# First batch of an attention + two-layer kernel written as one list of steps, with other load layouts, other PSUM places and regrouped norms for batches 1 and 2

## The chip, the cores and the metric

The kernel runs on one core of a Trainium2 chip. The metric is the device time of one execution in microseconds (us). Engines are named as in the profile: PE (TensorE), PEld (its weight loads), DVE (VectorE), ACT (ScalarE), POOL (GpSimd) and SP (SyncE, which here only issues DMAs). An engine takes its instructions strictly in the order in which the program lists them for that engine, and the kernel fixes that order by hand.

## What is computed

Eight batches of attention with 12 heads, 448 positions and head width 64, with q and k normalised by their root mean square, and after it two dense layers with a GELU between them:

```python
q_n, k_n = rmsnorm(q, g_q), rmsnorm(k, g_k)
attn = softmax(scale * q_n @ k_n.transpose(0, 1, 3, 2))
x = (attn @ v).transpose(0, 2, 1, 3).reshape(8 * 448, 768)
out = gelu_tanh(x @ w_in) @ w_out          # 768 -> 2048 -> 768
```

Inputs and outputs are float32 in HBM; the matmuls run in bf16.

## The kernel before, in words

**Tiling.** A batch's 12 heads are 6 pairs, and the pairs are 3 chunks of 4 heads (`c` = 0, 1, 2). Per chunk the kernel loads q and k (`load_q` L106, `load_k` L122, on SP's queue), squares them (`square` L164), sums the squares per row (`total` L192, DVE), takes the inverse root as exp(-0.5 ln) on ACT (`rsqrt` L195), multiplies (`normed` L209, on DVE or POOL) and transposes. A transpose is either four plus three or four TensorE transposes per pair (`trans` L221) whose results DVE copies out of PSUM, with k multiplied by the gains, or two DMA transposes per chunk (`dma_trans` L248) with a DVE multiply behind them (`gain` L260).

Keys are cut into 128-row tiles: three per head, and the last 64 keys of a head share a tile with another head's. So a pair has 3 score tiles, and each chunk one tile "r" more: 7 per chunk, 21 per batch. `scores` (L265) does two matmuls (four for "r") into a PSUM place of two banks, and one exp on ACT. There are three such places, which the first layer also uses. `pair_products` (L306) multiplies the exps by ones (what = 0, the softmax sums) and by v (what = 1); both write the single PSUM bank `o`. `pair_recips` (L326) turns the sums into reciprocals with two DVE transposes and a reciprocal, `pair_x` (L335) multiplies. For batches from 1 on, DVE first adds the exps of a pair (`key_sum` L291), so that the sums need 2 matmuls; for batch 0 they need 8.

The first layer (`mm1` L349) makes 16 blocks of 128 features in 6 steps each, two blocks to a PSUM place, with one GELU on ACT per place (L368). The second layer (`mm2` L376) runs in steps, 16 per output half tile; `attention` (L451) interleaves them as fills between the score tiles of the next batch, in 7 groups of three score tiles. After batch 0 there are 96 such steps, after later batches 112 on average.

**Order of the work.** `first_attention` (L514) runs batch 0's 21 score tiles with lists of side work per tile (L661 to L681). Its sums and products share the bank `o`, so that pair after pair goes sums, reciprocals, products, multiply. The transposes use the bank `mm`. Then come `first_blocks` (L496) and the rest of the first layer of batch 0; between them `between0` (L701) finishes batch 1's sums of squares, takes the inverse roots of the whole of batch 1 and loads the GELU table. Lines L713 to L720 norm batch 1 on DVE and transpose chunk 0 and chunk 2 on TensorE (`trans(1, 0)`, `trans(1, 1)`, `trans(1, 4)`, `trans(1, 5)`) and chunk 1 by DMA (`transposed(1, 1)`). In `attention(1)` POOL squares batch 2's chunks 1 and 2 and DVE sums those of all three (L721 to L727). The loop from L709 does the same for later batches, with POOL norming (`normed_all`) and DMA transposes for all chunks.

POOL's queue also issues the casting loads: v (`load_v` L139, six DMAs a batch), w_in in two parts (L609) and w_out in two halves (L615). SP's queue issues the q and k loads, the DMA transposes and the stores.

Of the kernel before, what the change touches and what calls it, by code (L numbers as in the profile page):

```python
# [16 lines left out]
def kernel(  # L17
# [34 lines left out]
    rawqk = ctx.enter_context(tc.tile_pool(name="rawqk", bufs=4))  # L52
    stp = ctx.enter_context(tc.tile_pool(name="stp", bufs=2))
    smp = ctx.enter_context(tc.tile_pool(name="smp", bufs=4))
    nrmp = ctx.enter_context(tc.tile_pool(name="nrmp", bufs=3))
# [6 lines left out]
    ps_s = ctx.enter_context(tc.tile_pool(name="ps_s", bufs=3, space=bass.MemoryType.PSUM))  # L62
    ps_o = ctx.enter_context(tc.tile_pool(name="ps_o", bufs=1, space=bass.MemoryType.PSUM))
    ps_m = ctx.enter_context(tc.tile_pool(name="ps_m", bufs=1, space=bass.MemoryType.PSUM))

# [21 lines left out]

    vb = [wts.tile([128, NCH, 2, NS, D], BF16, name=f"vb{i}") for i in range(2)]
    vr = [wts.tile([128, 2, NCH, 2, D], BF16, name=f"vr{i}") for i in range(2)]
# [27 lines left out]
    def halves(j):  # L117

        own, other = slice(64 * j, 64 * j + 64), slice(64 - 64 * j, 128 - 64 * j)
        return ((own, slice(0, 256), 4, 3 * j), (other, slice(256, S), 3, 4 * j))  # L120

    def load_k(b, c):  # L122
        t = rawqk.tile([128, 2, NS, D], F32, tag="rawk", name="rawk")
        raws["k", b, c] = t

        def go(j):
            h = head(c, j)
            for p, s, n, at in halves(j):
                nc.sync.dma_start(  # L129
                    t[p, :, at:at + n],  # L130
                    k[b, h:h + 2, s].rearrange("a (p t) d -> p a t d", t=n),
                )
        return [lambda j=j: go(j) for j in range(2)]

    def loads(b, c):
        for go in load_q(b, c) + load_k(b, c):
            go()

    def load_v(b, j, cs=slice(0, NCH)):  # L139
        src = v[b, HP * j + 2 * cs.start:HP * j + 2 * cs.stop]  # L140
        dst, rem = vb[b % 2], vr[b % 2]
        for p, s, n, at in halves(j):
            nc.gpsimd.dma_start(
                dst[p, cs, :, at:at + n].rearrange("p c a t d -> p (c a) (t d)"),
                src[:, s].rearrange("h (p t) d -> p h (t d)", t=n),
            )
        p, s, n, at = halves(j)[0]
        nc.gpsimd.dma_start(
            rem[p, j, cs].rearrange("p c a d -> p (c a) d"),
            src[:, s].rearrange("h (p t) d -> p h t d", t=n)[:, :, 3 - 3 * j],  # L150
        )
# [12 lines left out]
    def square(b, c, n, eng, part=None):  # L164
        if (n, b, c) not in sqs:
            sqs[n, b, c] = sq_tile(n, stp.tile([128, CH * NQ * D], F32, tag="sq", name="sq"))
# [54 lines left out]
    def trans(b, hp):  # L221

        c, j = hp // 2, hp % 2
        if hp == 0:
            qT[b] = qkp.tile([128, HP, S], BF16, tag="qT", name="qT")
        tp = ps_m.tile([128, 2, 512], BF16, tag="mm", name="tp")
        for t in range(NQ):
            nc.tensor.transpose(
                tp[:, 0, t * P:(t + 1) * P],
                nrms["q", b, c][:, j, t].rearrange("p a d -> p (a d)"), ident[:P, :P],  # L230
            )
        s = slots(j)
        n = s.stop - s.start
        for i in range(n):
            nc.tensor.transpose(
                tp[:, 1, i * 128:(i + 1) * 128],
                nrms["k", b, c][:, s.start + i].rearrange("p a d -> p (a d)"), ident,
            )
        if b == 0 and hp == 0:
            nc.scalar.copy(qT[b][:, hp], tp[:, 0, :S])  # L240
        else:
            nc.vector.tensor_copy(qT[b][:, hp], tp[:, 0, :S])
# [565 lines left out]
```

## Time and profile before

| what | us |
|---|---|
| three runs: median (lowest, highest) | 435.16 (433.12, 435.74) |
| the profiled execution | 437.02 |
| its span, first to last instruction | 434.9 |
| PE busy, share of the span | 414.1 (95%) |
| ACT, DVE, POOL busy | 286.1, 265.4, 160.6 |
| first score tile of batch 0 on PE | 9.10 |
| first matmul of the first layer, batch 0 | 39.55 |
| first score tile of batch 1 | 66.76 |
| start of the first layer of batch 1 | 101.24 |
| the same for batches 2 and 3 | 149.58, 197.92 |

The last five rows are read in the timeline of PE. They cut the run into stages: start, batch 0's attention, batch 0's first layer, batch 1's attention with batch 0's second layer inside, and then one period per batch. A period is 48.34 us long. A busy PE says little by itself, since fillers on zeros count as busy and a matmul at half the clock counts twice as long; the granted clock stands beside it.

### The profile page before, as it was taken

The page shows a single profiled execution, that of the slowest core. Times are in us where ns is not written, and L with a number is a line of the kernel's source. Part 1 is how long each engine was busy: PE and PEld are TensorE (multiplying, and loading weights), DVE is VectorE, ACT ScalarE, POOL GpSimd, SP SyncE. Part 2 cuts the span into 40 slices and gives each one's busy share as a digit, 9 for nine tenths or more (in the row PEclk, how much of TensorE's full clock was granted, in tenths as well). Part 3 has the DMA queues.
Part 4 walks back from the last instruction along what each step waited for, and adds up shares of the span by engine and source line. Part 5 has one row for each costly group of instructions (what it writes and reads, how often), then busy time and mean ns, then how long its engine had stood idle before and what let it go on. Part 6 is the DMA issues. An engine that isn't in the chain of part 4 may idle for free.

```text
span 434.9 us, 9265 instructions
## 1 busy us (share of the span) xinstructions
PE 414.1 (95%) x3776; PEld 236.4 (54%) x3776; DVE 265.4 (61%) x441; ACT 286.1 (66%) x382; POOL 160.6 (37%) x181
## 2 busy tenths in 40 slices
PE   8778798899999999999999999999999999999996
PEld 3234454456555565556465655556565655556563
DVE  5577846798667844787267845877377821784010
ACT  5676538366787758767786859777786648674400
POOL 4979223254660094205560194206560280000000
PEclk9899999699999999999999999999999999999999
DMA  7999999665895158913994168914991162120022
GB/s 177 217 228 233 231 179 230 124 110 95 206 194 107 38 128 170 217 51 73 208 186 102 38 150 160 217 43 78 220 142 39 38 110 56 36 69 7 2 72 72
DMA packets 90505, 54.92 MB, mean 126 GB/s; under 512 B 51808, under 2 KB 85472, under 8 KB 90464
## 3 DMA queue, kind: packets, MB, share of 16 engines
q1 hardware_dynamic: 65248, 41.67, 42.9%
q0 software_dynamic: 24896, 12.59, 21.9%
q8 instruction: 29, 0.48, 0.4%
q10 hardware_dynamic: 320, 0.10, 0.1%
q14 instruction: 12, 0.10, 0.1%
HBM read 47.19 MB, written 11.01 MB: 134 GB/s over the span
## 4 chain that ended last, share of the span: by engine, by line
PE 79%; DMA 13%; DVE 5%; SPq 2%; issue 1%; ACT 0%; DVEq 0%
PE o L386 32%; PE hh L362 26%; PE o L321 10%; PE sc L285 6%; DMA rawk<-in_k_dram 6%; DMA rawq<-in_q_dram 4%; PE h L362 3%; DMA kT<-nrmk 3%; PE sc L275 1%; SPq L129 1%; DVE ss L193 1%; DVE es L301 1%; DVE es L299 1%; SPq L110 1%; DVE nrmq L216 0%
## 5 line engine op out<-in xcount | busy, mean ns | idle before, releaser
L386 PE MATMUL o<-wout,g 128*64 128x384 bf16 (+1 forms) x1664 | 159.7, 329 | 0.0
L289 ACT ACTIVATE ex<-sc,shift 128x896 bf16<-128x896 f32 x144 | 136.6, 1013 | 8.5 <-PE sc L285 8.4
L362 PE MATMUL hh<-xT,win 128*64 128x448 bf16 (+1 forms) x960 | 135.3, 355 | 2.7 <-ACT g L368 2.6
L386 PEld LDWEIGHTS <-g 128*64 128x64 bf16 (+1 forms) x1664 | 99.4, 110 | 50.6 <-issue 4.6
L362 PEld LDWEIGHTS <-win 128*64 128x64 bf16 (+1 forms) x1098 | 88.1, 106 | 61.5 <-issue 8.2
L368 ACT ACTIVATE g<-hh 128x896 bf16<-128x896 f32 x56 | 49.6, 917 | 55.0 <-PE hh L362 55.0
L193 DVE TENSOR_REDUCE ss<-sq 112x16 f32<-112x1024 f32 (+4 forms) x44 | 46.8, 1077 | 39.9 <-ACT sq L176 32.7
L408 ACT COPY osb<-o 128x384 f32<-128x384 f32 x51 | 24.7, 485 | 59.5 <-PE o L386 59.5
L331 DVE STREAM_TRANSPOSE st<-o 128x448 f32<-128x448 f32 x48 | 31.2, 649 | 29.4 <-PE o L321 29.3
L654 POOL COPY mark<-es 1x1 bf16<-1x1 bf16 x6 | 1.1, 178 | 127.0 <-DVE es L301 127.0
L216 POOL TENSOR_TENSOR nrmq<-rawq,rinv 112x512 bf16<-112x512 f32 x40 | 41.7, 1060 | 3.1 <-ACT rinv L202 3.1
L285 PE MATMUL sc<-qT,kT 64*128 64x448 bf16 x288 | 38.6, 355 | 1.4 <-DVE kT L243 0.9
L321 PE MATMUL o<-ex,vb 128*64 128x448 bf16 x288 | 36.9, 363 | 1.0 <-DVE st L331 0.8
L301 DVE TENSOR_TENSOR es<-ex 128x896 bf16<-128x896 bf16 x42 | 27.7, 659 | 15.4 <-ACT ex L289 15.2
L216 POOL TENSOR_TENSOR nrmk<-rawk,rinv 128x384 bf16<-128x384 f32 (+1 forms) x40 | 36.8, 936 | 0.0
L338 DVE TENSOR_TENSOR xT<-o,rb 128x448 bf16<-128x448 f32 x48 | 29.6, 617 | 4.4 <-PE o L321 3.5
L178 POOL TENSOR_TENSOR sq<-rawq 112x1024 f32<-112x1024 f32 x9 | 17.4, 1929 | 39.9 <-DMA rawq<-in_q_dram 25.8
L333 DVE STREAM_TRANSPOSE rb<-rc 128x448 f32<-128x448 f32 x48 | 31.0, 645 | 1.6
L299 DVE TENSOR_TENSOR es<-es,exr 64x896 bf16<-64x896 bf16 x42 | 27.4, 653 | 3.0 <-ACT exr L289 1.6
L301 DVE TENSOR_TENSOR es<-es,ex 128x896 bf16<-128x896 bf16 x42 | 27.1, 645 | 2.4 <-ACT ex L289 0.3
L261 DVE TENSOR_SCALAR kT<-kT,gcol 128x896 bf16<-128x896 bf16 x19 | 15.4, 813 | 21.4 <-DMA kT<-nrmk 21.4
L289 ACT ACTIVATE exr<-sc,shift 128x896 bf16<-128x896 f32 x24 | 24.5, 1021 | 0.2 <-PE sc L275 0.2
(71 smaller groups left out, 318.4 us busy)
## 6 DMA issues: line engine op xcount, KB each, us to landing
rawq<-in_q_dram SPq DMA_DIRECT2D x48, 224.0 KB, 4.2
rawk<-in_k_dram SPq DMA_DIRECT2D x48, 128.0 KB, 4.5
rawk<-in_k_dram SPq DMA_DIRECT2D x48, 96.0 KB, 4.4
vb<-in_v_dram POOLq DMA_DIRECT2D x16, 192.0 KB, 6.0
win<-in_moe_w_in_dram POOLq DMA_DIRECT2D x2, 1536.0 KB, 16.9
wout<-in_moe_w_out_dram POOLq DMA_DIRECT2D x2, 1536.0 KB, 21.8
out_dram<-osb SPq DMA_DIRECT2D x7, 336.0 KB, 3.9
vb<-in_v_dram POOLq DMA_DIRECT2D x16, 144.0 KB, 6.7
```

Of the source, the lines that this page charges most:

```text
L193: nc.vector.reduce_sum(stat(ssq[b % 3], b, c, n, j), view(n, sqs[n, b, c], j), axis=AX.X)
L216: eng.tensor_mul(dst.rearrange("p t a d -> p a t d"), view(n, raws[n, b, c], j), r.to_broadcast(list(r.shape) + [D]),)
L285: nc.tensor.matmul(sc[:, a, :S], kT[r, c, 4 * j + t], qT[b][r, hp], start=True, stop=True,)
L289: nc.scalar.activation(dst, sc[:, :, :S], AF.Exp, scale=scale, bias=shift)
L299: nc.vector.tensor_add(es[p], es[p], exrs[b, hp // 2][p])
L301: nc.vector.tensor_add(es, ex[:, 0] if t == 1 else es, ex[:, t])
L321: nc.tensor.matmul(o[a * D:(a + 1) * D], w(a), e[:, a], start=(i == 0), stop=(i + 1 == len(steps)),)
L331: nc.vector.transpose(st.rearrange("p a b -> p (a b)"), oas[0])
L333: nc.vector.transpose(oas["rb"], rc.to_broadcast([128, S // 32, 32]))
L362: nc.tensor.matmul(h[i * m:(i + 1) * m, j, :S], win[:, c // 2 + NCH * (c % 2), f * 128 + i * m:f * 128 + (i + 1) * m], xT[b][:, c], start= ...
L368: nc.scalar.activation(g[:, fs[0]:fs[0] + len(fs), (b % 2) * S:(b % 2 + 1) * S], h[:, :, :S], AF.Gelu_apprx_tanh)
L386: nc.tensor.matmul(o[j * m:(j + 1) * m, :HD], g[:, f, i * 128 + j * m:i * 128 + (j + 1) * m], wout[:, f, half * HD:(half + 1) * HD], start ...
```

## The change

In batch 0 and up to the end of its first layer, the code that ordered the work (`first_attention`, its side lists, `between0`, the batch-0 lists L713 to L720) is replaced by one string of steps, `FRONT`, which a function `front` walks through. A step names its work and, after a colon, its engine (A, D, P for ACT, DVE, POOL). `s3` is the matmuls of score tile 3, `e3` its exp, `sq`/`sk` squares, `tq`/`tk` row sums, `rs` inverse roots, `nq`/`nk` norms, `tpq`/`tpk` transposes, `cq`/`ck` their copies out of PSUM, `su`, `st`, `rc`, `rb`, `xp`, `xt` a pair's sums, the three parts of the reciprocals, the products and the multiply, `ma`/`mc`/`md` parts of the first layer, `g` a GELU, `v`, `w`, `o`, `L` loads, and capitals the same for batch 1. `z` is filler matmuls.

- **PSUM.** Batch 0 has two score places instead of three; the other two banks take its q and k transposes (`tpq`, `tpk`). At step `U` these two banks become the third score place. Its products go to the bank `mm` and its sums to the bank `o`.
- **Loads.** k comes as 384 rows on 128 partitions (pieces of 768 bytes) and the last 64 rows on 64 partitions (pieces of 256 bytes); before it was 256 rows on 64 partitions (1024 bytes) and 192 on the other 64 (768 bytes). q is loaded as before. v takes three DMAs a batch instead of six. In POOL's queue v and both parts of w_in stand directly behind two small operations of the start. w_out comes in four parts.
- **Batch 1.** Inverse roots for chunks 0 and 1 are taken inside batch 0's first layer, between two more table loads; chunk 0 is transposed into the banks `o` and `mm`, chunk 1 into two score places (`TP2`, `TP3`) at the end of the first layer. Chunk 2's inverse roots come after it, its norms on DVE behind the first three score tiles of `attention(1)`, and its transposes by DMA, with `gain(1, 2)` at the end of group 3.
- **Batch 2.** Its squares, sums, inverse roots and norms move: chunk 0 squared by ACT in groups 5 and 6 of `attention(1)`, chunks 1 and 2 in batch 1's first layer, with two table loads and the inverse roots there; all norms on DVE. Batch 3's squares of chunks 1 and 2 go to ACT in `attention(2)`.
- **Pools.** Squares have four buffers of their own, norms two instead of three, the reciprocal's first transpose one instead of two.

```diff
-    nrmp = ctx.enter_context(tc.tile_pool(name="nrmp", bufs=3))
+    nrmp = ctx.enter_context(tc.tile_pool(name="nrmp", bufs=2))
-    ps_s = ctx.enter_context(tc.tile_pool(name="ps_s", bufs=3, space=bass.MemoryType.PSUM))
+    ps_s = ctx.enter_context(tc.tile_pool(name="ps_s", bufs=2, space=bass.MemoryType.PSUM))
+    ps_t = tc.tile_pool(name="ps_t", bufs=1, space=bass.MemoryType.PSUM)
+    turn = [ps_t.__enter__()]
...
+        def main(j):
+            h = head(c, j)
+            nc.sync.dma_start(
+                t[:, :, 4 * j:4 * j + NK],
+                k[b, h:h + 2, :SM].rearrange("a (p t) d -> p a t d", t=NK),
+            )
+        def last(j):
+            h = head(c, j)
+            nc.sync.dma_start(t[own(j), :, NK], k[b, h:h + 2, SM:].rearrange("a p d -> p a d"))
...
+    def third():
+        ps_t.__exit__(None, None, None)
+        pool = ctx.enter_context(tc.tile_pool(name="ps_u", bufs=1, space=bass.MemoryType.PSUM))
+        turn.extend([pool, ps_s, ps_s])
...
+        elif name == "TP":
+            tp = place("tp").rearrange("p a s -> p (a s)").bitcast(BF16)
+            tps["Q", i], tps["K", i] = (
+                trans(1, i, n, tp[:, 1024 * a:1024 * (a + 1)]) for a, n in enumerate("qk"))
...
+    FRONT = """
+        sq0:A tq0 sk0:A tk0 sq1:P gcol rs0 shift nq0:P tq1 sk1:A tk1 tpq0 sq2:A v0 nk0:D rs1 cq0:D
+        tpk0 tq2 sk2:A z3 v1 ck0:A tk2 v2 s0 nk1:D rs2 s1 w0 nq1:D e0 tpk1 sk3:D w1 tpq1 e1 s2 tk3
+        z5 sq3:P ck1:D e2 cq1:D nk2:P tq3 s3 sq4:A s4 nq2:D rs3 tpk2 e3 tq4 nq3:P tpq2 z1 ck2:D e4
+        cq2:D s5 nk3:D su0 e5 sk4:D L10 s6 tk4 sq5:P tpq3 e6 st0 tpk3 s7 sk5:P tq5 rs4 su1 rc0 e7
+        rb0 nk4:P s8 ck3:D nq4:P s9 e8 st1 tpk4 cq3:D xp0 e9 ck4:D tk5 tpq4 xt0 s10 rs5 s11 cq4:D
+        e10 xp1 nq5:P rc1 rb1 e11 s12 nk5:P xt1 su2 e12 L11 L12 s13 st2 tpq5 e13 tpk5 s14 rc2
+        Sk0:P xp2 ck5:D e14 rb2 s15 xt2 su3 cq5:A Sq0:P e15 U Tk0 s16 xp3 e16 st3 s17 rc3 Tq0 s18
+        e17 z403 rb3 e18 s19 su4 xt3 e19 s20 st4 xp4 e20 o0 rc4 rb4 ma0 GELU o1 xt4 Sq1:P su5 xp5
+        V0 V1 st5 V2 Sk1:P rc5 mc0 rb5 ma1 xt5 Tq1 o2 o3 md0 mc1 Tk1 g0 md1 ma2 g1 EXP mc2 md2 md3
+        Rs0 GELU Nq00:D Nk00:D Sk2:D g2 Tp0 md4 g3 Nk01:D Sq2:D Ck0:A Cq0:A Nk11:D md5 g4 Nq01:D
+        Tq2 Nk10:P Nq10:P Tk2 Tp1 g5 Nq11:P md6 Ck1:D Cq1:A md7 g6 TP2 Ck2:D Cq2:D md8 TP3 Ck3:D
+        Cq3:D g7 g8
+"""
+    for step in FRONT.split():
+        front(step)
...
+            here = {(0, 0): [lambda j=j, n=n: normed(1, 2, n, j, nc.vector)
+                             for j in range(2) for n in "qk"] +
+                            [lambda: transposed(1, 2)] +
+                            [lambda c=c: loads(2, c) for c in range(NCH)]}
+            late = [(3, lambda: gain(1, 2))]
...
+            m1.append((14, lambda: (nc.scalar.preload_act_table_set(EXP_SET),
+                                    rsqrt(2, slice(1, NCH)),
+                                    nc.scalar.preload_act_table_set(GELU_SET))))
```

## The prediction

> **What bounds the kernel now.** I read the busy times by stage first, then the chain that ended last, then PE's waits, then the DMA queues. The stages are cut at the marks of PE's timeline.
>
> ```profile
> 0.00:9.10 9.10, 7.14 (x32) 2.95 (x32) 4.33 (x17) 4.63 (x8) 3.02 (x14) 1.00 0.72 174
> 9.10:39.55 30.45, 23.36 (x182) 9.96 (x184) 20.48 (x41) 21.39 (x32) 27.35 (x29) 0.94 1.20 223
> 39.55:66.76 27.21, 23.70 (x181) 13.81 (x178) 19.00 (x32) 11.22 (x14) 10.73 (x12) 0.94 1.29 208
> 66.76:101.24 34.48, 30.38 (x299) 16.84 (x300) 27.72 (x41) 23.52 (x30) 11.66 (x10) 0.90 0.87 160
> 101.24:149.58 48.34, 48.34 (x474) 28.22 (x470) 35.46 (x52) 35.78 (x50) 19.10 (x21) 1.00 0.66 128
> 149.58:197.92 48.34, 48.34 (x474) 28.22 (x471) 31.05 (x52) 36.41 (x50) 19.22 (x21) 1.00 0.66 133
> ```
>
> Columns: window and length, then busy time of PE, PEld, DVE, ACT, POOL, PE's granted clock, DMA share, GB/s. From 101.24 on PE is busy for the whole period at clock 1.00, batch after batch. That part can only stay or get longer. All that can be gained lies ahead of 101.24, where PE idles and its clock falls below 1.00.
>
> ```profile
> 39.72 10.85 DMA rawk<-in_k_dram
> ...
> 55.51 14.46 DMA kT<-nrmk
> ...
> 70.00 0.46 DVE kT L261
> 70.45 2.12 DVE ss L193 x2
> ...
> 75.79 2.10 DVE es L299
> ...
> 77.94 0.59 PE o L321 x2
> ```
>
> The chain says how the loss arises: k of batch 1 lands late, its DMA transpose (chunk 1) takes 14.46 us, DVE stands behind it in `gain(1, 1)`, then sums batch 2's squares, and the key sums for batch 1's first pair come late.
>
> ```profile
> PE o L321 <- DVE es L299: 3.0, 2, 2.9
> PE hh L362 <- ACT g L368: 2.6, 1, 2.6
> PE tp L228 <- POOL nrmq L216: 1.7, 1, 1.7
> ```
>
> These are PE's longest waits before 101.24 (total, times, longest), and each leaves the clock low behind it, here the first:
>
> ```profile
> 75.10:77.94 2.84, 0.01 (x2) 0.01 (x2) 2.81 (x4) 2.64 (x3) 1.93 (x1) 0.79 1.13 240
> 77.94:84.50 6.56, 6.56 (x44) 3.50 (x46) 4.84 (x8) 0.03 (x1) 0.00 (x0) 0.57 0.70 145
> ```
>
> DMA between 17 and 50 us, shares of 16 engines:
>
> ```profile
> q0 software_dynamic: 3500, 4.09, 71.3%
> q1 hardware_dynamic: 4067, 3.54, 45.6%
> ```
>
> POOL's weights and SP's q and k loads both want the engines all the time, move about equally many packets, and SP's queue gets 3.54 MB in 33 us, 107 GB/s.
>
> **The change, part by part.** Four stages change.
>
> *Batch 0's attention, start to first matmul of the first layer (before: 39.55).* First the start. In the new list DVE does `tq1` and `tk1` ahead of `nk0`, and `tk1` needs pair 1's k, which is complete with the sixth of SP's DMAs, 0.6 us of issue each. I put the first exp at 11.3 by walking the chain (sixth landing 6.5, square 0.63, sum 0.69, norm 0.55, transposes and copy 1.1, inverse roots of pairs 1 and 2 on ACT in between) against 9.50 in the timeline: 1.8 later. From there ACT has 21 exps, three of which took 2.91 in a row (0.97 each): 20.4. Between them stand `sq4` 0.63, three inverse roots of 0.53 and one copy of 0.53: 2.8. That ends at 34.5 if ACT never waits; before, its last exp ended at 40.3, and ACT waited 8.4 us for score tiles in eight places. DVE has from 10.7 on six half sums (0.67), two whole ones (1.07, 1.18), four norms (0.69), two squares which it did not do before (0.65, estimated from its norms of the same size), nine PSUM copies (0.42), five reciprocals (0.65 + 0.24 + 0.65) and five multiplies (0.62): 24.9, ending at 35.6. So both engines carry about the same, and separate banks for transposes, sums and products let PE deliver early. What is late next is `Tk0` on DVE: it needs POOL's square of batch 1's chunk 0, whose load (`L10`) reuses the buffer of batch 0's chunk 1 and so waits for `nk3`, at about 18. Chunk loads of 0.92 MB take 8.6 us at 107 GB/s, so `Tk0` can be 2 us late. I take 36.5, a gain of **3.0**. Ends: 33.0 (no wait) and 39.55 (the waits are kept).
>
> *Batch 0's first layer (27.21).* PE's own work: 96 matmuls at 9.19/48 = 0.191: 18.4; sums and products of pair 5, 0.95 each: 1.9; four pairs' transposes 0.4 each: 1.6; together 21.9. Before, sums and products of pair 4 lay here too, with the 2.57 wait for `g` (ACT was held by the inverse roots of all of batch 1). New are two table loads of 1.28 and 0.65 for inverse roots on ACT. PE has three places of 2.3 us work in front of that, so it is hidden; if that cover is gone it costs up to 3.2. A wait is added for DVE: `Sk2` needs chunk 2 of batch 1, and behind it stand `Nk01`, `Nk11`, `Nq01`, on which `Tp1` on PE waits. Transposing chunk 1 on PE in two score places costs the same 0.4 per pair that chunk 2 cost. I add 1.8 for stalls: 23.7, a gain of **3.5**. Ends: 21.9 and 28.2.
>
> *Batch 1's attention (34.48).* In a steady period the attention takes 48.34 - 18.45 = 29.9 with 112 second-layer steps. Sixteen steps are 1.14 + 1.46 = 2.6, so with 96 steps 27.3 is the floor, and 7.2 is lost now: 2.84 in the wait, 2.8 from 6.56 us at clock 0.57, 1.5 in small waits. Gone are the two sums on DVE (2.12), the wait for chunk 1's DMA transpose and POOL's squares beside DVE: `es` took 2.1 with POOL busy, 0.62 without. New are the 0.65 for chunk 2's inverse roots ahead of the exps and four norms (2.5) on DVE behind the first tiles. Group 2's sums need tile "r": exps start 2.6 after the stage's first tile, six exps and a copy make 8.5, one add 9.2, and PE is there at 8.1: a wait of 1.1 remains. With 1.0 for clock and 0.5 for the rest I take 29.9, a gain of **4.5**. Ends: 27.3 and 33.0 (the old wait with its clock, without the sums).
>
> On the clock, gaps of 1.7, 2.6 and 2.84 us were all followed by 4 to 7 us at 0.57 to 0.66, so a gap of 1.1 lies just under the rows. The Trainium skill, TensorE: Matmul & The Clock Gate, section Why this matters for your kernels, puts the limit for gaps at about 3 us; by it the 1.0 would be none and the stage 28.9. The trace disagrees, since the 1.7 us gap was enough; I keep the row.
>
> *Batches 1 and 2 after that.* In batch 1's first layer ACT gets squares of batch 2 (0.95, 1.05), two table loads and 0.65. In the old run's time, with blocks 0 to 5 and 14 evaluated by 113.2 (0.92 each behind PE's 109.2, and one square), the tables and roots push the GELU of blocks 6 and 7 to 117.3, and PE wants their place for blocks 12 and 13 at 116.7: a wait of 0.6; with the later first exp I take a **loss of 1.0**. Ends: 0 and 4. The eight half squares in `attention(2)` (0.6 each) fill ACT: per group three exps 2.9, copy 0.49, two halves 1.1, 4.5 against 4.6 of PE. That is hidden with nothing to spare.
>
> *At nothing, with their cover.* Batch 2's loads stand in SP's queue behind chunk 2's transposes; the first who needs them is a square in group 5 of `attention(1)`, some 17 us later, and if they land after it, ACT's exps behind that square wait. v in three DMAs instead of six takes 2 us off POOL a batch, behind PE's full period. Norms in two buffers hold POOL's third chunk until chunk 0's DMA transpose lands (median 3.3 and 3.0 us after 100): about 2 us of POOL, with chunk 2's scores 16 us away. k in 384 pieces instead of 256 adds a quarter to a chunk's pieces; after 101.24 the DMA share is 0.66, so it is hidden; before, see the rivals. Moving both w_in parts from 18.8 and 28.7 to about 10 in POOL's queue brings them 9 to 18 us earlier and costs SP's loads their share.
>
> Sum: -3.0 - 3.5 - 4.5 + 1.0 = -10.0. The profiled execution is 437.02, 1.86 over the median 435.16, with a span of 434.9 and 2.1 around it. I predict 427.0 for it and **425.2** for the median.
>
> **The rivals.**
>
> *Half of it is given back at the loads.* If SP's queue gets packets rather than bytes, its chunk takes (448 + 768) / (448 + 512) = 1.27 times as long while weights are queued: batch 1's chunk 2 lands near 50 instead of 46.6, DVE stands in `Sk2` from 45 to 50, and `Tp1` holds PE for 3; stage one loses 2 more. That gives 425.2 + 5 = 430.2. For it: the equal packet counts, and 48 KB in pieces of 256 bytes took 10.0 us to land, 192 KB in pieces of 1024 took 7.9. Against: the last landing moves less than the pieces do. The Trainium skill, DMA: Bandwidth & Descriptors, section Specifications, says that pieces under 512 bytes miss line rate; the v rows agree in direction.
>
> *No change.* `gain(1, 2)` stands at the end of group 3 on DVE. Its k transpose is issued some 6.5 after the stage's start. At 3.0 it is in time, at 14.46, as now, it lands at 21, 4.5 late for group 4 at 16.5, and the clock costs 2.8 more: 425.2 + 7.3 = 432.5. For it: the DMA share of 1.29 just before. Against: the weights are issued earlier, so the engines should be free by then.
>
> *Slower.* Batch 0's chunk 2 loads (issued at 8 to 12) now share with all of w_in. `sq4` stands in ACT's queue ahead of `e3` and needs its q at 14.3. Under weights a q load took 15.8; times 1.27 it lands 20.1 after 8.2, at 28.3, 14 late, and everything shifts: 425.2 + 14 = 439.2. It decides from a landing about 16 after issue, where the gain of 10 is gone. For it: 15.79 us for rawq from 23.9 in the chain. Against: the quickest q load of the run landed in 2.4, and before the change POOL found chunk 2's q ready at 19.7 without a wait, with all of v in the queues.
>
> **How the numbers follow.** The forecast gets 0.62, with its own range of 418 to 429 (part of the ends together). The loads' rival gets 0.18, no change 0.12, slower 0.08. The range 417 to 433 takes in the low end of the sum short of all ends at once (-19) and reaches over the first two rivals; the slower case stays outside. About 1% is what a measurement of this kernel tells from no change, so faster means under 430.8: nearly all of the forecast, most of the first rival, a little of the second: 0.79. Within 1%: 0.13. Slower: 0.08.
>
> **What would show it.** The first matmul of the first layer at 36 to 37; the first tile of batch 1's attention near 60; the start of batch 1's first layer near 90; no wait over 1.5 us of PE in that attention, and clock 1.00 in it; periods of 48.34 from batch 2 on. DVE idle before `Sk2`'s square on a DMA would speak for the first rival, DVE idle before `kT` of `gain` for the second, ACT idle before a square at 14 on a DMA for the third. The prediction is wrong at its root if a period after batch 2 grows.

## The result and the profile after

| | before | after |
|---|---|---|
| median of 4 runs each, side by side | 435.45 (433.12 to 437.11) | 429.32 (428.68 to 430.6) |
| profiled execution; its span | 437.02; 434.9 | 429.53; 427.8 |

The ratio is 0.9875 (not the quotient of the two medians), 95% interval 0.9841 to 0.9909. (Ratios here and below leave out an execution that took over 1.5% longer than the fastest of the same kernel.) By the medians the kernel is 6.1 us faster, where 10 were forecast: 429.32 lies in the range 417 to 433, 4 us above 425.2. It is nearly the time of the first rival, 430.2.

The busy times of the changed kernel by stage, with the columns of the first fence of the prediction and cut at the same marks (the last row ends 0.24 behind its mark):

```profile
0.00:10.49 10.49, 7.50 (x31) 3.02 (x32) 5.50 (x19) 5.52 (x11) 7.05 (x18) 1.00 0.80 193
10.49:41.08 30.59, 23.43 (x175) 9.30 (x176) 25.28 (x43) 22.29 (x31) 18.89 (x17) 0.89 1.19 227
41.08:63.08 22.00, 21.76 (x144) 11.63 (x143) 15.27 (x20) 13.07 (x18) 15.99 (x13) 1.00 1.38 202
63.08:91.87 28.79, 27.60 (x301) 15.56 (x301) 22.21 (x42) 24.11 (x33) 0.00 (x0) 1.00 0.92 201
91.87:142.50 50.63, 49.15 (x477) 28.67 (x474) 42.12 (x70) 42.92 (x58) 9.55 (x8) 1.00 0.64 122
```

| change of the time in a stage | forecast | this profile |
|---|---|---|
| I: start to the first layer's first matmul | -3.0 | +1.5 (41.08 for 39.55) |
| II: batch 0's first layer | -3.5 | -5.2 (22.00 for 27.21) |
| III: batch 1's attention | -4.5 | -5.7 (28.79 for 34.48) |
| IV: the next two periods (start of the first layer of batches 1, 2, 3: 91.87, 142.26, 190.86) | +1.0 | +2.3 (50.39 and 48.60 for 48.34 each) |
| sum | -10.0 | -7.1 (spans: 427.8 for 434.9) |

Stages II and III gave 2.9 more than forecast and stage IV cost 1.3 more. The shortfall is in stage I, the one that the change rewrote most: it is 4.5 off. Its chain of waits (start, length, what) says why:

```profile
16.21 16.88 DMA rawk<-in_k_dram
...
33.21 1.69 POOL sq L183
...
34.92 1.09 DVE ss L198
36.01 0.57 DVE st L356
...
36.62 1.28 PE o L212 x3
```

The last DMA of batch 1's first chunk of k, issued at 16.21, takes 16.88 us to land. POOL's square, DVE's row sum `Tk0` and the first part of pair 3's reciprocal (`st3`, behind `Tk0` on DVE) follow it without a gap, and PE waits for the last of them. The timelines of POOL, DVE and PE show the three waits at the ends of these lines:

```profile
33.21 1.68 POOL L183 TENSOR_TENSOR sq<-rawk 128x896 f32<-128x896 f32 x1 [4.46 <-DMA rawk<-in_k_dram]
```

```profile
34.92 1.09 DVE L198 TENSOR_REDUCE ss<-sq 128x14 f32<-128x896 f32 x1 [2.84 <-POOL sq L183]
```

```profile
36.62 1.28 PE L212 MATMUL o<-zeros 128*128 128x448 bf16 x3 [2.25 <-DVE st L356]
```

No single wait of PE is over 2.3 us up to 100 us, and the 2.84 for `es` with its low clock behind it is gone: in batch 1's attention the clock is 1.00 (0.90 before), and the waits there are 0.5, 0.4 and 0.3.

The DMA queues, cut finer than in the prediction, explain the landing. Queue, packets, MB, share of 16 engines; the changed kernel from 18 to 26 and from 26 to 34 us:

```profile
q0 software_dynamic: 941, 1.17, 83.0%
q1 hardware_dynamic: 908, 0.67, 34.2%
```

```profile
q0 software_dynamic: 665, 1.33, 87.4%
q1 hardware_dynamic: 663, 0.46, 24.1%
```

The kernel before, from 18 to 26:

```profile
q1 hardware_dynamic: 1345, 1.19, 68.4%
q0 software_dynamic: 1314, 0.62, 57.9%
```

In all three stretches the two queues move about the same number of packets, whatever these hold (941 and 908, 665 and 663, 1345 and 1314). Ahead of 18 us that does not hold: from 12 to 16 the changed kernel's q0 moved 1241 packets and q1 535. A packet of POOL's queue holds 1.24 KB in the first, 2.0 KB in the second and 0.47 KB in the third, because v stood there before and w_in stands there now. From 18 to 34 SP's queue so gets 1.13 MB, 71 GB/s, where the prediction's stretch of 17 to 50 us of the old run had given 107. The Trainium skill (DMA: Bandwidth & Descriptors, section Queues, rings and completion order) says that each DMA engine takes the queues in turn, a packet at a time, where a packet is typically some 9 to 17 descriptors (single pieces of a transfer). The packets that the rows count are smaller, one row of w_in each from 26 us on; their equal numbers from 18 us on fit such turns without showing how long one is, and those from 12 to 16 do not fit.

### The profile page after: what moved, and what is told of

The parts are those of the page before. It is cut to its first block, busy times and chain, and to the rows that moved or that the text cites. A ratio compares the mean times of both kernels' runs of the same rounds, so it can differ in the third digit from the quotient of the medians.

```text
span 427.8 us, 9133 instructions
## 1 busy us (share of the span) xinstructions
PE 410.6 (96%) x3733; PEld 232.7 (54%) x3733; DVE 279.0 (65%) x452; ACT 296.8 (69%) x400; POOL 133.7 (31%) x139
## 4 chain that ended last, share of the span: by engine, by line
PE 81%; DMA 7%; ACT 5%; DVE 5%; issue 1%; SPq 1%; POOL 0%; DVEq 0%; ACTq 0%; POOLq 0%
PE o L418 33%; PE hh L391 25%; PE o L349 10%; DMA rawk<-in_k_dram 7%; PE sc L312 6%; PE h L391 4%; PE sc L302 1%; ACT g L400 1%; ACT ex L316 1%; DVE ss L198 1%; DVE sq L183 1%; ACT exr L316 1%; DVE es L328 1%; ACT sq L181 1%; DVE st L356 1%
## 5 line engine op out<-in xcount | busy, mean ns | idle before, releaser
L418 PE MATMUL o<-wout,g 128*64 128x384 bf16 (+1 forms) x1664 | 157.8, 326 | 0.0
L391 PE MATMUL hh<-xT,win 128*64 128x448 bf16 (+1 forms) x924 | 133.2, 353 | 0.1
L391 PEld LDWEIGHTS <-win 128*64 128x64 bf16 (+1 forms) x1062 | 86.2, 105 | 59.1 <-issue 3.6
L198 DVE TENSOR_REDUCE ss<-sq 128x14 f32<-128x896 f32 (+2 forms) x43 | 47.4, 1124 | 30.4 <-ACT sq L181 18.5
L221 POOL TENSOR_TENSOR nrmq<-rawq,rinv 112x512 bf16<-112x512 f32 x36 | 38.8, 1093 | 6.0 <-ACT rinv L207 6.0
L349 PE MATMUL o<-ex,vb 128*64 128x448 bf16 x252 | 31.2, 353 | 1.2 <-DVE st L356 1.2
L274 DVE TENSOR_SCALAR kT<-kT,gcol 128x896 bf16<-128x896 bf16 x19 | 21.8, 1146 | 13.4 <-DMA kT<-nrmk 13.4
L330 DVE TENSOR_TENSOR es<-es,ex 128x896 bf16<-128x896 bf16 x42 | 25.6, 609 | 2.6 <-ACT ex L316 0.7
L374 DVE TENSOR_TENSOR xT<-o,rb 128x448 bf16<-128x448 f32 x42 | 25.9, 616 | 0.7
L312 PEld LDWEIGHTS <-kT 64*128 64x128 bf16 x288 | 10.1, 94 | 25.1 <-issue 19.3
```

Of the source, the lines that this page charges most:

```text
L198: nc.vector.reduce_sum(stat(ssq[b % 3], b, c, n, j), view(n, sqs[n, b, c], j), axis=AX.X)
L221: eng.tensor_mul(dst.rearrange("p t a d -> p a t d"), view(n, raws[n, b, c], j), r.to_broadcast(list(r.shape) + [D]),)
L312: nc.tensor.matmul(sc[:, a, :S], kT[r, c, 4 * j + t], qT[b][r, hp], start=True, stop=True,)
L330: nc.vector.tensor_add(es, ex[:, 0] if t == 1 else es, ex[:, t])
L349: nc.tensor.matmul(o[a * D:(a + 1) * D], w(a), e[:, a], start=(i == 0), stop=(i + 1 == len(steps)),)
L391: nc.tensor.matmul(h[i * m:(i + 1) * m, j, :S], win[:, c // 2 + NCH * (c % 2), f * 128 + i * m:f * 128 + (i + 1) * m], xT[b][:, c], start= ...
```

## The experiments

The theory after the result: stage I waits at `Tk0` for the load of batch 1's first chunk, and that load is late because w_in, put ahead, takes its share of the DMA engines. The wait is read from the chain; the reason for the late load is argued from the queues' rows. Rivals: the many ops of two inputs on DVE and POOL hold each other up; the new pieces of k are slow; the buffer of the load comes free late, as the prediction had it. For stages III and IV: what exactly was gained by transposing chunk 1 on TensorE and by POOL's absence, and which engine lengthens batch 1's period.

Each profiled execution, with the marks that the reading needs. "Square" is the start of POOL's square of batch 1's first k chunk, "layer" the first matmul of the first layer, "tile" the first score tile of batch 1, "rest" the time less "tile". Ratios are to the kernel before, with 95% intervals.

| variant | square | layer | tile | time | rest | median | ratio |
|---|---|---|---|---|---|---|---|
| changed kernel | 33.21 | 41.08 | 63.08 | 429.53 | 366.45 | 429.32 | 0.9875 (0.9841, 0.9909) |
| the same again | 28.17 | 35.65 | 59.24 | 425.89 | 366.65 | 430.55 | 0.9872 (0.9827, 0.9917) |
| sums later | 33.74 | 34.10 | 62.65 | 429.09 | 366.44 | 426.40 | 0.9815 (0.9792, 0.9838) |
| weights later | 27.91 | 35.91 | 59.07 | 425.99 | 366.92 | 426.06 | 0.9813 (0.9777, 0.9848) |
| squares on ACT | 33.44 | 41.65 | 63.65 | 430.29 | 366.64 | 430.59 | 0.9894 (0.9872, 0.9916) |
| chunk 1 by DMA | 34.56 | 43.29 | 64.51 | 436.24 | 371.73 | 430.95 | 0.9891 (0.986, 0.9922) |
| old pieces | 31.33 | 38.33 | 60.24 | 427.99 | 367.75 | 429.44 | 0.9873 (0.9829, 0.9917) |
| POOL squares, early | 34.45 | 42.56 | 65.57 | 432.27 | 366.70 | 431.01 | 0.9895 (0.9857, 0.9934) |
| batch 2's sums earlier | 28.59 | 35.76 | 59.53 | 426.63 | 367.10 | 427.71 | 0.9836 (0.9788, 0.9884) |
| sums and weights later | 29.15 | 37.14 | 60.69 | 427.35 | 366.66 | 427.35 | 0.9813 (0.9788, 0.9839) |
| and DVE's squares later | 28.83 | 36.47 | 59.63 | 426.39 | 366.76 | 426.28 | 0.9795 (0.9764, 0.9827) |
| POOL beside the sums | 34.82 | 42.74 | 64.74 | 434.56 | 369.82 | 433.56 | 0.9952 (0.9922, 0.9982) |
| one spare buffer (the same program) | 36.45 | 44.34 | 66.34 | 433.08 | 366.74 | 431.19 | 0.9904 (0.9867, 0.9941) |

Two things stand out before any single run is read. "Rest" is 366.4 to 367.1 in ten of the thirteen rows: what the executions differ in is almost all ahead of batch 1's first tile. And there "tile" follows "square" at a distance of 28.9 to 31.5, over a span of squares from 27.9 to 36.5: the time of the kernel goes with when the first k chunk of batch 1 lands.

**The sums of batch 1's first chunk later.** They no longer stand ahead of `st3`.

```diff
-        Sk0:P xp2 ck5:D e14 rb2 s15 xt2 su3 cq5:A Sq0:P e15 U Tk0 s16 xp3 e16 st3 s17 rc3 Tq0 s18
+        Sk0:P xp2 ck5:D e14 rb2 s15 xt2 su3 cq5:A Sq0:P e15 U s16 xp3 e16 st3 s17 rc3 s18
...
-        V0 V1 st5 V2 Sk1:P rc5 mc0 rb5 ma1 xt5 Tq1 o2 ...
+        V0 V1 st5 V2 Sk1:P rc5 mc0 rb5 ma1 xt5 Tk0 Tq0 Tq1 o2 ...
```

> The changed kernel with DVE's two sums of batch 1's chunk 0 (Tk0, Tq0) moved behind the last multiply of batch 0, nothing else. Theory A (the first layer started late because Tk0 made DVE wait for POOL's square and so for a load): st3 no longer stands behind it, the first matmul of the first layer comes 3 to 4 us earlier (37 to 38 against 41.1) and the run gains 2.5 to 3.5 us on the changed kernel. Theory B (the stage is late because DVE and POOL hold each other up from 11 to 21): the first layer starts within 1 us of where it did and the run gains under 1.

Measured 426.40 (426.26 to 429.09). The profiled execution was one in which the load landed late again (33.74), and yet the first layer began at 34.10, 7 us earlier. Most of that is given back in the first layer, by windows:

```profile
10.81:34.10 23.29, 20.57 (x175) 8.98 (x175) 20.35 (x41) 21.64 (x31) 11.24 (x12) 1.00 1.20 221
34.10:62.65 28.55, 24.79 (x144) 12.61 (x142) 17.67 (x22) 13.32 (x18) 22.39 (x17) 0.88 1.32 215
```

```profile
PE tp L233 <- DVE nrmq L221: 4.2, 3, 3.8
```

So the wait at `Tk0` is what held stage I. Behind it stands the same late load by another way: the norms that PE then waits for need the inverse roots of chunks 0 and 1, which are taken together, and the last of their squares is chunk 1's on POOL:

```profile
44.56 1.72 POOL L183 TENSOR_TENSOR sq<-rawk 128x896 f32<-128x896 f32 x1
```

It stands in POOL's list behind chunk 0's squares, which had waited for the load, and behind the issues of w_out and v. Moving the wait alone gained 0.4 in this execution. Why the median came down by more is not seen in it; four of the six executions took 426.3 to 426.5, about the time of the traced ones with an early landing, but they were not traced.

**The second half of w_in later.** `w1` goes behind `nq4` and is issued at 23.6 instead of 11.5.

```diff
-        ... tpk1 sk3:D w1 tpq1 e1 s2 tk3
+        ... tpk1 sk3:D tpq1 e1 s2 tk3
...
-        rb0 nk4:P s8 ck3:D nq4:P s9 e8 ...
+        rb0 nk4:P s8 ck3:D nq4:P w1 s9 e8 ...
```

> The changed kernel with the second part of w_in issued behind the norms of pair 4 on POOL (near 24 us) instead of at 11.5. Theory A' (the weights take the load queue's share): batch 1's chunk 0 lands 3 to 5 us earlier than 33.2, DVE's wait before Tk0 (2.8 us) shrinks under 1, the first layer starts near 38.5. Rival: SP's queue is paced by its own packets or by buffers, the load lands within 1 us of 33.2 and nothing is gained; if w_in then lands after 48 the second half of the first layer waits and the run loses.

Measured 426.06 (425.61 to 430.66), five of six executions at 426.3 or less. The square began at 27.91, without a wait, the first layer at 35.91. But the weights did not move later, so the reason given ahead of the run is not what happened. Issue to landing of that half in the changed kernel:

```profile
win<-in_moe_w_in_dram POOLq DMA_DIRECT2D x1, 1536.0 KB, 29.2
```

With the edit, and the queues from 18 to 26 us:

```profile
q0 software_dynamic: 1090, 1.10, 81.1%
q1 hardware_dynamic: 1079, 0.73, 38.6%
...
win<-in_moe_w_in_dram POOLq DMA_DIRECT2D x1, 1536.0 KB, 16.9
```

Issued at 11.5 or at 23.6, the second half lands near 40.5: the first half is ahead of it in POOL's queue and lands near 31 in both. POOL's queue moved nearly as much as before (1.10 MB for 1.17, then 1.30 for 1.33 from 26 to 34). SP's queue was ahead earlier, with 1.68 MB from 8 to 18 us against 1.47; how the edit would do that is not shown. No run put the first half of w_in back, which is the half that shares the engines with this load. What is late next is chunk 2's k: DVE stands 2.5 us before `Sk2`, which is the place that the first rival had named:

```profile
DVE sq L183 <- DMA rawk<-in_k_dram: 2.5, 1, 2.5
```

**The changed kernel once more.** This run, made later, limits how much the last one proves.

> The changed kernel once more, unedited. In its profile Tk0 waited for a load of k that landed at 33.2, and the first layer began at 41.1; in a variant with the same code up to there the load had landed by 28.6 and the first layer began at 35.8. If the landing of that load differs between executions of the same code, this profile has the first layer's start anywhere in 35.5 to 42, and the times spread over 426 to 431, single runs near 426 among them. If the 41.1 is fixed by the code, the start is within 0.5 of 41.1 and every time is 428.5 to 431.

Measured 430.55 (425.89 to 431.78). The fastest of its six executions was the profiled one, and in it the unedited kernel does what the prediction said: the first layer starts at 35.65, DVE and PE do not wait for `Tk0`'s load, the first layer takes 23.59 (forecast 23.7).

```profile
28.17 1.68 POOL L183 TENSOR_TENSOR sq<-rawk 128x896 f32<-128x896 f32 x1 [0.71 <-issue]
```

```profile
10.70:35.65 24.95, 21.89 (x176) 9.07 (x176) 23.36 (x43) 21.70 (x31) 16.19 (x16) 0.93 1.21 227
35.65:59.24 23.59, 21.76 (x144) 11.63 (x143) 13.95 (x20) 13.43 (x18) 13.82 (x13) 1.00 1.32 212
```

What is late in it is chunk 2's k, in stage II:

```profile
49.28 1.09 DVE L183 TENSOR_TENSOR sq<-rawk 128x896 f32<-128x896 f32 x1 [2.84 <-DMA rawk<-in_k_dram]
```

The same code so lands the same load at 28 or at 33, and at 36 in a third trace (below, with one spare buffer). From 18 to 34 us SP's queue moved 1.31 MB here (1129 packets against 1149, then 650 against 652) and 1.13 above; the equal turns hold in both, but with more packets left of v's small ones in the first stretch. The changed kernel had sixteen executions, that third trace's six among them: one took 425.89, the others 428.27 to 433.08, and the median of all is 430.2. With w_in's second half later it was five of six below 426.3. The three traced kernels with this edit (two follow) have the square at 27.91, 29.15 and 28.83; of the other ten in the table two have it before 29.2. So the later issue goes with the early landing. That it is the cause is likely, not shown, and by which way is open.

**Both.** The two edits together.

> The changed kernel with both edits that helped: DVE's sums of batch 1's chunk 0 behind the last multiply, and the second part of w_in behind pair 4's norms. The first edit alone started the first layer at 34.1 and then lost most of it again to batch 1's later loads, the second alone brought these loads 5 us earlier. If the loads of batch 1 are the bound, both together gain more than either: first layer at 33 to 34, attention of batch 1 at 57 to 58, 424 to 425 us. If the edits remove the same wait twice, it stays within 0.7 us of 426.

Measured 427.35 (427.0 to 427.46): no more than either alone, as two remedies for one wait should. DVE waits 2.3 for chunk 2's k at `Sk2`, and PE 1.7 for a norm of q behind it.

**And DVE's squares of chunk 2 behind the norms.**

```diff
-        Rs0 GELU Nq00:D Nk00:D Sk2:D g2 Tp0 md4 g3 Nk01:D Sq2:D Ck0:A Cq0:A Nk11:D md5 g4 Nq01:D
+        Rs0 GELU Nq00:D Nk00:D g2 Tp0 md4 g3 Nk01:D Ck0:A Cq0:A Nq01:D md5 g4 Nk11:D Sk2:D Sq2:D
```

> Sums of batch 1's chunk 0 behind the end of batch 0, weights behind the q and k loads, and besides the squares Sk2 and Sq2 on DVE behind the norms Nk01, Nq01 and Nk11. Theory: with the first wait gone, DVE stands in Sk2 (2.3 us) and PE in the transposes of pair 1 (1.7 us) behind it; with the squares behind the norms this wait of PE is gone, the first layer's stage goes from 23.6 to about 22, the kernel to 425 to 426.5. Rival: the inverse roots of chunk 2 then come late and PE waits for chunk 2's norms or DVE for its transposes in batch 1's attention: within 0.7 of the 427.35 of the version with the squares ahead.

Measured 426.28 (425.48 to 427.24), side by side with the changed kernel's 430.55. The wait of DVE for the load is gone, chunk 2 is in time:

```profile
49.27 0.68 DVE L221 TENSOR_TENSOR nrmk<-rawk,rinv 128x512 bf16<-128x512 f32 x1
49.87 1.93 DVE L183 TENSOR_TENSOR sq<-rawk 128x896 f32<-128x896 f32 x1
```

but the squares now take 1.93 and 2.06 beside POOL's norms (1.09 and 1.22 in the changed kernel's second trace), and the copy of pair 1's k comes behind them and chunk 2's sums. PE waits for it, and the first layer took 23.16, not 22:

```profile
56.48 1.29 PE L391 MATMUL h<-xT,win 128*128 128x448 bf16 x6 [1.34 <-DVE kT L259]
```

Beside the version without this edit (ratio 0.9813) nothing is proved; beside the changed kernel it is the best version here, 4 us faster, and its slowest execution is faster than fifteen of the sixteen of the changed kernel.

**Squares of batch 0 on ACT.** `sq3` and `sq5` move from POOL to ACT, so that POOL has less to do beside DVE.

```diff
-        z5 sq3:P ck1:D e2 ...
+        z5 sq3:A ck1:D e2 ...
...
-        ... tk4 sq5:P tpq3 e6 st0 ...
+        ... tk4 tpq3 e6 sq5:A st0 ...
```

> The changed kernel with the q squares of pairs 3 and 5 on ACT, which idled there, instead of POOL. Theory B: DVE's norm at 11.7 (2.24 us) falls to 0.7 and the norm and square at 18.3 and 19.8 (1.5, 1.4) to 0.7 and 0.6; the exps up to number 15 come 2 to 3 us earlier. The wait for the load of batch 1's chunk 0 is then longer by as much, so theory A expects the first layer to start within 0.7 us of 41.1 and the run within 0.7 us of the changed kernel; theory B alone would give 38.5 and 2.5 us.

Measured 430.59 (428.99 to 431.61). DVE's stretched ops are back at their length (a norm of q that took 2.24 at 11.72 takes 0.68), batch 0's work comes to `Tk0` some 3 us earlier, and all of it turns into a longer wait there, now the longest of PE:

```profile
36.84 1.28 PE L212 MATMUL o<-zeros 128*128 128x448 bf16 x3 [5.70 <-DVE st L356]
```

The first layer starts at 41.65, as before the edit. Two engines holding each other up is real and costs nothing here: the load bounds.

**The old pieces of k and v.**

```diff
+    def halves(j):
+        other = slice(64 - 64 * j, 128 - 64 * j)
+        return ((own(j), slice(0, 256), 4, 3 * j), (other, slice(256, S), 3, 4 * j))
...
-        return [lambda: main(0), lambda: main(1), lambda: last(0), lambda: last(1)]
+            for p, s, n, at in halves(j):
+                nc.sync.dma_start(
+                    t[p, :, at:at + n],
+                    k[b, h:h + 2, s].rearrange("a (p t) d -> p a t d", t=n),
+                )
```

> The changed kernel with k and v loaded as before the change (k in pieces of 1024 and 768 bytes, v in six DMAs of the same split), all else as changed. If the pieces of 256 bytes slow the loads under the weights (the rival of the prediction), batch 1's chunk 0 lands at 29 to 31 instead of 33.2, the first layer starts 2 to 4 us earlier than 41.1 and the run gains 1.5 to 3 us. If bytes are what counts, it lands within 1 us of 33.2 and the run stays within 1 us of the changed kernel, or loses some tenths by three more DMAs on POOL ahead of w_in.

Measured 429.44 (427.35 to 432.9), the changed kernel's time. The square started at 31.33, inside the spread of the kernel with the new pieces. The 256-byte pieces, one half of the first rival's case, are not shown to cost anything; its other half, turns by packets, is what the queues show.

**One spare buffer.** It was meant to let the load of batch 1's first chunk reuse a buffer that is free at 14, not 18.

```diff
-    for _ in range(2):
-        rawqk.tile([P, CH, NQ, D], F32, tag="rawq", name="rawq")
-        rawqk.tile([128, 2, NS, D], F32, tag="rawk", name="rawk")
+    rawqk.tile([P, CH, NQ, D], F32, tag="rawq", name="rawq")
+    rawqk.tile([128, 2, NS, D], F32, tag="rawk", name="rawk")
```

> One spare raw buffer at the start instead of two, so that the load of batch 1's chunk 0 reuses the buffer of batch 0's chunk 0 (free at about 14) and not that of chunk 1 (free at about 18). Buffer theory: the load is issued 3 to 4 us earlier, lands 3 us earlier, the first layer starts 2 to 3 us earlier and the kernel takes 426 to 427.5. Queue theory: what lies ahead of the load in SP's queue and the weights beside it set its landing: it lands within 1 us of the changed kernel's, and the kernel is within 1 us of it.

Measured 431.19 (429.12 to 433.08), the changed kernel's 430.55 beside it. The edit has no effect: both kernels issue the same instructions with the same waits, and the load of this chunk waits for no buffer in either. Its six DMAs are issued from 12.34 to 16.8 in the changed kernel and from 12.41 to 17.7 here, right behind those of batch 0's third chunk (the last of them at 16.21, when the load eight places ahead of it has landed); only the next chunk's wait for a buffer. Both theories had taken over the prediction's error that the load stands until 18. So the run is a third trace of the same program, with the latest landing of all:

```profile
36.45 1.68 POOL L183 TENSOR_TENSOR sq<-rawk 128x896 f32<-128x896 f32 x1 [7.94 <-DMA rawk<-in_k_dram]
```

The load is on its way for some 21 us in the changed kernel's first trace and 24 in this one, and what moves beside it is the likely reason. This run rules the buffer out by the issue times; what it says of queues is only that the spread is wider, 28 to 36.

**Chunk 1 by DMA again.** Its transposes on TensorE undone, all else kept; `gain(1, 1)` at the end of group 1.

```diff
-        Tq2 Nk10:P Nq10:P Tk2 Tp1 g5 Nq11:P md6 Ck1:D Cq1:A md7 g6 TP2 Ck2:D Cq2:D md8 TP3 Ck3:D
-        Cq3:D g7 g8
+        Tq2 Nk10:P Nq10:P Tk2 Tp1 g5 Nq11:P D11 md6 Ck1:D Cq1:A md7 g6 md8 g7 g8
...
+            early = [(1, lambda: gain(1, 1))]
```

> The changed kernel with batch 1's chunk 1 transposed by DMA again (issued when its norms are done, gain in group 1 of batch 1's attention) instead of on TensorE in score places. If the queues are still full at 58 to 65, its k transpose takes 10 to 14 us, DVE waits for it in group 1, and PE's wait before the first sums grows by 2 to 4 us with clock lost behind it: 3 to 6 us slower than the changed kernel. If the queues are nearly empty by then it lands in 3 to 4 us and, with 0.8 us of transposes off PE, the run is 0.5 to 1 us faster.

Measured 430.95 (427.48 to 436.24), by the times not to be told from the changed kernel's 430.2. The profiled execution, at 436.24, is the slowest of the six and the only one traced: its rows show how such a transpose can cost, not that it does in most executions. The transpose of k took 10.87 us in a stretch where POOL's queue moves the last of w_out and a load of v (2746 packets from 61 to 73 us; 47 from 67 to 72 in the changed kernel). DVE stood before the norms of chunk 2 whose buffers the transposes read, PE waited 4.3 for the k behind them, and the attention took 33.98 again:

```profile
68.78 0.69 DVE L221 TENSOR_TENSOR nrmq<-rawq,rinv 112x512 bf16<-112x512 f32 x1 [6.88 <-DMA qT<-nrmq]
72.73 0.56 DVE L221 TENSOR_TENSOR nrmk<-rawk,rinv 128x384 bf16<-128x384 f32 x1 [3.26 <-DMA kT<-nrmk]
```

In the changed kernel the only DMA transposes of this stage are chunk 2's, issued at 67.1 and 68.6; `gain(1, 2)` finds them landed, with no wait beside it:

```profile
80.25 0.44 DVE L274 TENSOR_SCALAR kT<-kT,gcol 128x896 bf16<-128x896 bf16 x1
```

**POOL's squares beside the key sums,** first try: two useless squares of raw data in group 1 of batch 1's attention.

```diff
+            def extra(n):
+                t = sq_tile(n, sqp.tile([128, CH * NQ * D], F32, tag="sq", name="sq"))
+                nc.gpsimd.tensor_mul(t, raws[n, 1, 2], raws[n, 1, 2])
+            side = [(1, lambda: extra("q"), lambda: extra("k"))]
```

> The changed kernel with two squares more on POOL in group 1 of batch 1's attention, of batch 1's last chunk into a spare buffer, as work that nobody needs: it puts back what POOL did there before. If DVE is held up by POOL, key sums that took 0.62 take 1.5 to 2.3 us, PE's wait before the first sums grows from 0.3 to 1.5 to 3 us, the clock falls below 0.7 behind it, and the stage of 28.8 becomes 31 to 34. If POOL does not matter, the stage stays within 0.5 of 28.8 and the old wait came from the sums and the DMA transpose alone.

Measured 431.01 (429.13 to 432.27). Inconclusive: nothing held POOL back, and the squares ran at 59.06 and 61.37, ahead of the stage that begins at 65.57. `es` stayed at 0.62 and the stage at 28.78.

Second try: POOL first waits for the first key sum, by the `gpsimd_waits` that the kernel has.

```diff
+            side = [(1, lambda: gpsimd_waits(ess[1, 0][:1, 0, :1]),
+                     lambda: extra("q"), lambda: extra("k"))]
```

> Two useless squares on POOL that start when the first key sum of batch 1's first pair is written, so that they lie beside the following key sums on DVE. Theory (POOL's square beside DVE's adds is what made a key sum take 2.1 us before the change): es goes from 0.62 to between 1.5 and 2.3 for one or two of them, PE's wait for the first sums from 0.3 to 1.5 to 3, with a lower clock behind it, and the attention stage from 28.8 to between 31 and 34, the kernel 2 to 5 us slower. Rival (only DVE's own two sums of squares and the wait for the transposed k stood in the way before): es stays under 0.8, the stage within 0.5 of 28.8 and the kernel within 1 us.

Measured 433.56 (429.28 to 434.6). The squares lie from 70.72 to 74.24, and in DVE's timeline one key sum, 0.63 in the changed kernel, becomes 2.38:

```profile
69.89 0.62 DVE L330 TENSOR_TENSOR es<-es,ex 128x896 bf16<-128x896 bf16 x1
72.35 2.38 DVE L330 TENSOR_TENSOR es<-ex 128x896 bf16<-128x896 bf16 x1 [1.83 <-ACT ex L316]
```

PE's wait for it, and the clock behind that:

```profile
75.31 0.38 PE L349 MATMUL o<-es,ones 128*64 128x448 bf16 x2 [1.69 <-DVE es L328]
```

```profile
76.60:80.50 3.90, 3.90 (x34) 2.18 (x30) 2.55 (x5) 0.00 (x0) 0.01 (x1) 0.68 1.01 152
```

The stage took 31.85 for 28.79, 3.1 more: 1.4 in the wait, and most of the rest at the clock of 0.68. By this, and if the old squares lay as these do, taking them out of the stage is worth about 3 of the 5.7, an estimate. The Trainium skill (GPSIMD Engine Reference, section 1. Specifications) says that POOL shares its SBUF interfaces with DVE and contends with DVE instructions of two SBUF inputs; the key sum is one, and the row agrees.

**Batch 2's first sums earlier.** The squares move from groups 5 and 6 to 3 and 4, the sums to 4 and 5, to take DVE's sums out of the seam behind batch 1's attention.

```diff
-            late += [(5 + "qk".index(n), lambda n=n, half=half: squared(2, 0, n, half))
+            late += [(3 + "qk".index(n), lambda n=n, half=half: squared(2, 0, n, half))
...
-            late += [(5, lambda: total(2, 0, "q", 0)), (6, lambda: total(2, 0, "q", 1)),
-                     (6, lambda: total(2, 0, "k"))]
+            late += [(4, lambda: total(2, 0, "q", 0)), (4, lambda: total(2, 0, "q", 1)),
+                     (5, lambda: total(2, 0, "k"))]
```

> The changed kernel with batch 2's chunk 0 squared in groups 3 and 4 of batch 1's attention instead of 5 and 6, and its row sums in groups 4 and 5. If the 2.3 us lost between 91.9 and the later periods come from DVE doing these sums just ahead of reciprocals, the wait of 0.6 at 96 goes and this period falls from 50.4 to 49.3 to 49.9: a gain of 0.5 to 1. If the table loads on ACT are the cause, the period stays within 0.2 of 50.4.

Measured 427.71 (426.29 to 432.86); its profiled execution had the early landing, which is why it is fast. Read by stage, the edit moves the cost:

```profile
59.53:89.33 29.80, 27.82 (x300) 15.87 (x300) 23.69 (x44) 25.64 (x36) 0.00 (x0) 1.00 1.03 218
89.33:139.29 49.96, 48.73 (x473) 28.51 (x470) 41.07 (x67) 41.29 (x56) 9.55 (x8) 1.00 0.64 121
```

The period is 0.43 shorter (50.39 before the edit), the attention 1.0 longer (28.79). In the period the wait behind batch 2's sums is gone, and PE now waits 0.48 for ACT's GELU, which is the wait that the prediction had named there.

## Why the prediction was partly right

**Stage I is where it failed.** The step that failed is "Chunk loads of 0.92 MB take 8.6 us at 107 GB/s, so `Tk0` can be 2 us late. I take 36.5". The place was right, and the two halves of the price were wrong. The load does not wait for `nk3`: it is issued from 12.34 on. And it does not take 8.6 us: its last DMA landed at 33.1, 20.8 us after the issue of its first. The 107 was a mean over 17 to 50 us of a run whose POOL queue still held v's small packets from 18 to 26 (0.47 KB each); with w_in in front SP's queue gets 71 from 18 to 34, and it carries more than this chunk then. 41.08 came of it, 35.65 where the load landed early, and 44.34 in the third trace. In the early one the stage's other numbers hold: the last exp ends at 36.1 (forecast 34.5 if ACT never waits); the first began at 11.26 in the changed kernel's first profile (forecast 11.3). With the wait moved away and the load as late as before, the layer began at 34.10, near the forecast's end without a wait, 33.0. So the work of both engines was counted well, and the landing is a spread, of which the forecast took the better side. Why the load comes early or late stays open. The upper end, 39.55, was passed too: it allowed for the old waits to stay, not for a later load.

**Stage II**, 23.7: 23.59 with the early landing and 22.00 with the late one, against a floor of 21.9. These are one thing: a late start lets the loads catch up, so that I and II together differ by 3.8 (63.08 and 59.24), not by 5.4. The 1.7 that stage II gave beyond its forecast is the other side of the late landing, and it hides part of what stage I lost: that the sum came within 3 us is partly luck. The two table loads are hidden as forecast (48.62 to 51.84, no wait of PE there over 0.2). Of the 1.8 for stalls PE shows 1.8 in one wait with the early landing, for a norm of q behind `Sk2`.

**Stage III**, 29.9: 28.79. The floor of 27.3 plus 1.2 in waits of PE. The 1.0 for the clock did not come, since no wait there was longer than 0.5: the forecast wait of 1.1 for the sums of group 2 was 0.3. The prediction set against this the limit of about 3 us for gaps that the Trainium skill has (TensorE: Matmul & The Clock Gate, section Why this matters for your kernels), by which the stage was 28.9. The time is near that, but the gap that would have tested it did not occur. The added gap of 1.69 in the experiment was followed by 3.9 us at 0.68, and in the changed kernel one of 1.76, ended at 22.33, by 4.1 us at 0.58; both speak against 3 us as the limit, as the row of 1.7 did.

**Stage IV**, +1.0: +2.3, and by another engine. The forecast had ACT push the GELU of blocks 6 and 7; PE has no wait for `g` in that period. It waits 0.6, 0.2 and 0.6 for DVE, the first of them behind batch 2's row sums:

```profile
94.36 1.67 DVE L198 TENSOR_REDUCE ss<-sq 112x8 f32<-112x512 f32 x2
95.94 0.64 DVE L356 STREAM_TRANSPOSE st<-o 128x448 f32<-128x448 f32 x1
```

```profile
96.64 0.76 PE L349 MATMUL o<-ex,vb 128*64 128x448 bf16 x6 [0.61 <-DVE st L356]
```

Another 0.6 of the 2.05 in this period lies in matmuls of longer total (48.91 busy for 48.34). The prediction costed the squares of batch 2 on ACT and left out that the sums on DVE stand ahead of a pair's reciprocal.

**The rivals.** The loads' rival had equal packets and DVE late behind a load, which the rows bear out, and by the median the right time (430.2; measured 429.32, 430.55 and 431.19, and 430.2 over all sixteen executions). That time is partly luck. It took its price from the pieces of 256 bytes, and undoing these changed nothing that could be measured; what grew in the rows is POOL's packets. And it put 3 of its 5 us at `Sk2`, where the traces show a wait (2.84) only if `Tk0` did not wait. A chance of 0.18 was still too little for it. The no-change rival is out: chunk 2's transposes landed in 3.3 and 2.9 us and `gain(1, 2)` did not wait, though `D11` shows how long such a transpose took 7 us earlier in one execution. The slower one is out: ACT waited for no load in stage I in the first trace, and 0.4 us in the second.

## What to carry to other kernels

When a bulk load is moved forward in one DMA queue, price the other queue's transfers by equal packets against it, not by the bytes per second of a stretch in which the first queue held small packets; then look whether the first instruction that waits for such a transfer stands in an engine's list ahead of work that is ready. Removing such a wait may only show the next consumer of the same load: here it brought the first layer 7 us forward and the kernel 0.4. When an edit helps, look in its trace whether it did what it was meant to do: w_in's second half, issued 12 us later, landed when it had before. Where times of one kernel spread by more than a per cent, trace it twice and find the mark from which on the executions agree.

## What was not expected of the hardware

- In three executions of one program the load of the same 0.9 MB chunk let its square start at 28.17, 33.21 and 36.45; these 8.3 us are 7.1 at batch 1's first tile (59.24 and 66.34) and 7.2 in the time (425.89 and 433.08). What sets the one or the other was not found; SP's queue had moved more in the early case from 8 to 18 us already (1.64 MB against 1.47 and 1.28), in which v, ahead of w_in in POOL's queue, and the q and k loads compete.
- In these rows DVE and POOL instructions of two inputs take turns rather than share time: a key sum of 0.63 became 2.38 beside POOL's two squares, and ended 0.5 after the second. Where the load was late, such turns cost the kernel nothing that could be measured (squares on ACT: 430.59).
